# A state-space block with a gated MLP: the residual's addition given to accumulating DMAs, and the sums of one layer norm moved

## The chip, the cores and the metric

The kernel runs on one core of a Trainium2 chip. The metric is the device time of one execution in microseconds (us). A core has five engines with a queue each, which execute in order and meet through semaphores: TensorE (PE in the profile: matmuls, with weight loads PEld), VectorE (DVE), ScalarE (ACT), GpSimd (POOL), and SyncE (SP), which here only issues DMAs. Matmuls write PSUM, a small memory which the other engines must empty; all else lies in SBUF.

## The reference

The input x has 2048 rows of 512. It is normalized, and the normalized rows feed a diagonal complex recurrence with 512 states and a gated MLP of width 1792; the result is the sum of x and both branches.

```python
xn = _layernorm(x)                      # over 512, eps 1e-5, no gain
dt = exp(log_dt); Lam_bar = exp(dt * Lam)
B_bar = ((Lam_bar - 1.0) / Lam)[:, None] * Bmat
Bu = einsum("bld,pd->blp", xn, B_bar)
h[t] = Lam_bar * h[t - 1] + Bu[t]       # 2048 steps, complex
ssm = 2.0 * einsum("blp,dp->bld", h, Cmat).real + xn * Dskip
mlp = (silu(xn @ w1) * (xn @ w3)) @ w2
return x + ssm + mlp                    # bfloat16, [1, 2048, 512]
```

## The kernel before

The 2048 rows are cut into four blocks of 512 (four tiles of 128 rows each, `cl` 0 to 3). For each block b the work is:

- layer norm: rows of `x_blk[b]` become `xn_blk[b]`, and DMA transposes on SP (`ln_transpose`, L239) make `xnT_blk[b]` from it. There are three forms. Block 0 and block 1 use DVE; blocks 2 and 3 use ACT (`ln_scalar_engine`, L259): for each of the four row tiles a sum of x (`total`, L269), a sum of squared deviations (`squares`, L274) and the normalization (`norm`, L282). ACT's instructions give the sums through an accumulator, but each also has an elementwise result, which goes into the place of xn and is overwritten later. POOL makes the mean from the sums (L271), and then the reciprocal deviation (L277 to L279).
- `bu(b)`: 32 matmuls into two PSUM tiles in turn (`bu_ps`), each evacuated by ACT (L424) for the scans.
- `ssm_tasks(b)`: on DVE, a rotation, eight scans (L456) and a rotation back.
- `glu(b)`: 14 pairs of a gate and an up tile (L497, four PSUM tiles `gu_ps`), evacuated by ACT (L506, L507) and multiplied by DVE (L514).
- `res_tasks(b)`: on DVE, xn times Dskip (`mul`, L590), plus x (`add`, L594), in place of xn, and for blocks 1 to 3 a `difference` (L598), which the fast output needs.
- the output: for block 0 `y(0)`, whose four PSUM tiles are first seeded with the residual by ACT (`y_seed`, L749), then filled by `from_gate` (L756) and `from_state` (L762), and copied and stored by `finish` (L768, L769). Blocks 1 to 3 use `y_fast` (L674), a seven-product scheme on pairs of row tiles, which takes sums of activations made by DVE (`row_sums`, L649), and is seeded by ACT (`seeds`, L671).

The order on each engine is the order in which the Python code emits instructions; no scheduler reorders them. Two queues decide at emission what is interleaved. `bg`, a `Filler`, holds DVE work as (cost, function, key); `bg.fill(budget)`, called after matmuls, emits tasks as far as the budget goes, and `bg.flush(key)` emits all up to the last with this key. `sins` holds single ACT operations, and `sin_step()` emits one of them; the calls stand in `bu` (L425) and once in each pair of `glu` (L581).

Before the change, `ln_scalar_engine(2)` is emitted all at once ahead of `y(0)`; `ln_scalar_engine(3, sins)` puts its twelve ACT operations into `sins` behind `y(0)`, so that they are taken one by one in bu(2) and in the pairs of glu(2). The buffer of xn for a block is allocated (`ln_alloc`) at that call, out of three; the one for block 3 is that of block 0, which `y(0)` stores from.

PSUM is fully dealt out: four `gu_ps`, two `bu_ps` and two `y_ps` tiles of 512 float32 columns. `y_ps` serves the first transposes and, from output pair 1 on, half of the fast outputs.

Of the kernel before, what the change touches and what calls it, by code (L numbers as in the profile page):

```python
# [11 lines left out]
ALU = mybir.AluOpType  # L12
ACT = mybir.ActivationFunctionType

FP32 = DT.float32
BF16 = DT.bfloat16
FP16 = DT.float16
P = 128
# [44 lines left out]
def kernel(  # L63
# [17 lines left out]
    nc = tc.nc  # L81
    _, S, D = A_x.shape
# [16 lines left out]
    FAST = (1, 2, 3)  # L99
# [18 lines left out]
    ps_y = ctx.enter_context(tc.tile_pool(name="ps_y", bufs=2, space=bass.MemoryType.PSUM))  # L118
# [24 lines left out]
    x_blk = [xpool.tile([P, CPB, D], BF16, name="x_blk") for _ in range(NBLK)]  # L143
# [59 lines left out]
    bg = Filler()  # L203


    xn_blk = [None] * NBLK
# [12 lines left out]
    def ln_alloc(b):  # L219
        xn_blk[b] = lnp.tile([P, CPB, D], BF16, name="xn", bufs=3)  # L220
        xnT_blk[b] = xtp.tile([P, NDT, TBLK], BF16, name="xnT")
# [16 lines left out]
    def ln_transpose(b, cl):  # L238
        nc.sync.dma_start_transpose(out=xnT_blk[b][:, :, cl * P:(cl + 1) * P], in_=xn_blk[b][:, cl, :])  # L239
# [18 lines left out]

    def ln_scalar_engine(b, spread=None):  # L259

        ln_alloc(b)
        acc = lnp.tile([P, 4, CPB], FP32, name="acc")
        sm, nm, ss, nb = (acc[:, i, :] for i in range(4))
        rstd = rstd_all[:, b * CPB:(b + 1) * CPB]
        xn, gp = xn_blk[b], nc.gpsimd
        todo = []

        def total(cl):
            nc.scalar.activation(out=xn[:, cl, :], in_=x_blk[b][:, cl, :], func=ACT.Copy, accum_out=sm[:, cl:cl + 1])  # L269
            if cl == CPB - 1:  # L270
                gp.tensor_scalar(out=nm, in0=sm, scalar1=-1.0 / D, scalar2=None, op0=ALU.mult)  # L271

        def squares(cl):
            nc.scalar.activation(out=xn[:, cl, :], in_=x_blk[b][:, cl, :], func=ACT.Square, bias=nm[:, cl:cl + 1],  # L274
                                 scale=1.0, accum_out=ss[:, cl:cl + 1])
            if cl == CPB - 1:
                gp.tensor_scalar(out=ss, in0=ss, scalar1=1.0 / D, scalar2=LN_EPS, op0=ALU.mult, op1=ALU.add)  # L277
                gp.tensor_tensor(out=rstd, in0=ss, in1=mhalf, op=ALU.pow)
                gp.tensor_tensor(out=nb, in0=nm, in1=rstd, op=ALU.mult)  # L279

        def norm(cl):
            nc.scalar.activation(out=xn[:, cl, :], in_=x_blk[b][:, cl, :], func=ACT.Identity,  # L282
                                 bias=nb[:, cl:cl + 1], scale=rstd[:, cl:cl + 1])
            ln_transpose(b, cl)

        for fn in (total, squares, norm):
            for cl in range(CPB):
                if spread is None:
                    fn(cl)
                else:  # L290
                    spread.append((None, lambda fn=fn, cl=cl: fn(cl)))
# [13 lines left out]
    gp = nc.gpsimd  # L305
# [25 lines left out]
    sins = deque()  # L331
    sins_done = set()

    def sin_step(until=None):
        while sins and (until is None or until not in sins_done):
            key, fn = sins.popleft()
            fn()
            sins_done.add(key)
            if until is None:
                break  # L340
# [55 lines left out]
    def k_gate(f):  # L396
        return f if f < NFH else NK + f - NFH
# [4 lines left out]
    def act(b):  # L402
        if act_blk[b] is None:
            act_blk[b] = actp.tile([P, 2 * NK, TBLK], FP16, name="act")
        return act_blk[b]
# [7 lines left out]
    def bu(b):  # L413
        for hf in range(NPT // 2):
            u = up.tile([P, 2, 2, TBLK], BF16, name="u")
            u_blk[b, hf] = u
            for j in range(2):
                pt = 2 * hf + j
                for ri in range(2):
                    ps = ps_bu.tile([P, TBLK], FP32, name="bu_ps")  # L420
                    for dt in range(NDT):
                        nc.tensor.matmul(out=ps, lhsT=bt[:, ri, dt, pt * P:(pt + 1) * P], rhs=xnT_blk[b][:, dt, :],  # L422
                                         start=(dt == 0), stop=(dt == NDT - 1))
                    nc.scalar.activation(out=u[:, j, ri, :], in_=ps, func=ACT.Copy)  # L424
                if (b == 0 and pt > 0) or b == 1 or (b == 2 and pt > 1):  # L425
                    sin_step()
            bg.fill(3.4)

# [159 lines left out]
    def res_tasks(b):  # L588
        def mul():
            nc.vector.tensor_tensor(out=xn_blk[b], in0=xn_blk[b],  # L590
                                    in1=dskip_row[:, None, :].to_broadcast([P, CPB, D]), op=ALU.mult)

        def add():
            nc.vector.tensor_tensor(out=xn_blk[b], in0=xn_blk[b], in1=x_blk[b], op=ALU.add)  # L594

        def difference():
            o = xn_blk[b]
            nc.vector.tensor_tensor(out=o[:, 0::2, D2].bitcast(FP16), in0=o[:, 0::2, D2], in1=o[:, 1::2, D2],  # L598
                                    op=ALU.subtract)

        bg.add(1.2, mul)
        bg.add(1.2, add, ("res", b))
        if b in FAST:
            bg.add(0.4, difference, ("res", b))

    def weight_state(kh, dsl):
        return ct[:, kh * NPH:(kh + 1) * NPH, :, dsl].rearrange("p a r d -> p (a r) d")
# [22 lines left out]
    def sum_homes():  # L630
        n = NK * P
        flat = [bt.rearrange("p r t d -> p (r t d)"), w1_sb.rearrange("p t f -> p (t f)"),
                w3_sb.rearrange("p t f -> p (t f)")]
        b0, b1, a0, a1, a2, a3 = (v[:, i * n:(i + 1) * n] for v, m in zip(flat, (2, 2, 2)) for i in range(m))
        xs = [x_blk[i].rearrange("p c d -> p (c d)")[:, 0:n] for i in range(2)]
        q = flat[0][:, 2 * n:2 * n + 4 * DH].bitcast(FP32).rearrange("p (i d) -> p i d", d=DH)
        q_last = flat[1][:, 4 * n:4 * n + 2 * DH].bitcast(FP32)
        return [xs, [b0, b1], [b0, b1], [a0, a1], [a2, a3], xs], q, q_last
# [3 lines left out]
    def row_sums(n, b, p):  # L642
        a = act(b)
        r1, r2 = slice(2 * p * P, (2 * p + 1) * P), slice((2 * p + 1) * P, (2 * p + 2) * P)
        a11, a12 = a[:, 0:NK, r1], a[:, NK:2 * NK, r1]
        a21, a22 = a[:, 0:NK, r2], a[:, NK:2 * NK, r2]
        s1, s2 = (v.bitcast(FP16).rearrange("p (k t) -> p k t", t=P) for v in homes[n])
        sums[n] = dict(a11=a11, a12=a12, a22=a22, s1=s1, s2=s2, s3=a21)
        return [(0.9, lambda out=out, x=x, z=z, op=op: nc.vector.tensor_tensor(out=out, in0=x, in1=z, op=op), ("sums", n))  # L649
                for out, x, z, op in ((s1, a21, a22, ALU.add), (a21, a11, a21, ALU.subtract),  # L650
                                      (s2, s1, a11, ALU.subtract))]
# [99 lines left out]
    def y(b):  # L751
        tiles = y_tiles

        def from_gate(cl):
            for f in range(NFT):
                nc.tensor.matmul(out=tiles[cl], lhsT=act_blk[b][:, k_gate(f), cl * P:(cl + 1) * P],  # L756
                                 rhs=w2_sb[:, f, :], start=False, stop=False, skip_group_check=True)

        def from_state(cl):
            for ri in range(2):  # L760
                for pt in range(NPT):
                    nc.tensor.matmul(out=tiles[cl], lhsT=act_blk[b][:, k_state(pt, ri), cl * P:(cl + 1) * P],  # L762
                                     rhs=ct[:, pt, ri, :], start=False, stop=(ri == 1 and pt == NPT - 1),
                                     skip_group_check=True)

        def finish(cl):
            o = xn_blk[b][:, cl, :]
            nc.scalar.activation(out=o, in_=tiles[cl], func=ACT.Copy)  # L768
            nc.sync.dma_start(out=ov[:, b * CPB + cl, :], in_=o)  # L769

        for cl in range(0, CPB, 2):
            from_gate(cl)
            bg.fill(3.2)
            from_gate(cl + 1)
            bg.fill(3.2)
            if cl == 0:
                bg.flush(("ssm", b))
            from_state(cl)
            finish(cl)
            bg.fill(1.6)  # L780
            from_state(cl + 1)
            finish(cl + 1)
            bg.fill(1.6)
# [33 lines left out]
    y_seed(0, 2)  # L817
    y_seed(0, 3)
    ln_scalar_engine(2)
    y(0)  # L820
    pairs = [(b, p) for b in FAST for p in range(CPB // 2)]
    homes, q, q_last = sum_homes()
    for t in row_sums(0, *pairs[0]):
        bg.add(*t)
    ssm_tasks(2)
    ln_scalar_engine(3, sins)
    bu(2)
    gate = glu(2)
    gate()
# [4 lines left out]
    posts = ssm_tasks(3, True)  # L834
    y_fast(0, row_sums(1, *pairs[1]))
    y_fast(1, row_sums(2, *pairs[2]))
    posts()
    res_tasks(3)
    gate = glu(3)
    gate()  # L840
    bg.settle()
# [36 lines left out]
```

## Time and profile before

| | |
|---|---|
| median of 8 runs | 208.81 us (208.16 to 209.84) |
| the profiled execution | 208.84 us |
| its span | 207.0 us, so 1.84 us lie around it |
| granted TensorE clock | 1.00 |
| TensorE / DVE / ACT / POOL busy | 201.2 / 181.6 / 128.9 / 25.5 us |
| matmuls with 512 columns | 0.217 us each where they follow one another |

Times in the views are us from the start of the span. A timeline line gives the start, the length, the engine, the line of the code, the operation, out<-in, the number of merged instructions, and in brackets how long the engine had been idle before it and what ended that. A line of the waits gives who waited for whom, the total, the number of times and the longest. Rows last longer than the distance between starts, since instructions overlap at their ends.

The course of the span: block 0's layer norm, bu and glu up to 63 us with glu(1) at its end; bu(1) from 63.2; output 0 from 70.5 to 89.7; bu(2) from 89.9; glu(2) from 96.8; bu(3) from 122.2; the first two fast outputs from 129.1; glu(3) from 145.9; the last four fast outputs from 170.1.

### The profile page before, as it was taken

How to read it: one execution, taken by the hardware profiler on the slowest of the kernel's cores; microseconds unless marked ns; L12 is line 12 of the kernel's file. 1: busy time of each engine (PE TensorE's matmuls, PEld its weight loads, DVE VectorE, ACT ScalarE, POOL GpSimd, SP SyncE). 2: the span in 40 equal slices, each digit the busy share in tenths (PEclk: the TensorE clock that was granted, in tenths of full speed). 3: DMA queues.
4: the chain of work that ended last, by engine and by line, in shares of the span. 5: the costliest groups of instructions: out<-in, count | busy, mean ns of one | idle time of the engine just before them, and what ended most of it. 6: DMA issues, size and time to landing. Idle time of an engine off the chain costs nothing.

```text
span 207.0 us, 3249 instructions
## 1 busy us (share of the span) xinstructions
PE 201.2 (97%) x1251; PEld 115.8 (56%) x1251; DVE 181.6 (88%) x236; ACT 128.9 (62%) x257; POOL 25.5 (12%) x47
## 2 busy tenths in 40 slices
PE   8999999999999999999997999999999999999994
PEld 2774444444444444444443444888544458888893
DVE  3789699999997899999996889896999999996932
ACT  3799788699999984558995986300466672011010
POOL 3250289300000014000006000000000000000000
DMA  6999997930000000540000410000100000101011
GB/s 173 261 277 191 319 176 176 302 136 0 0 3 0 0 0 0 79 127 2 0 0 0 79 25 0 0 30 24 52 3 0 0 0 3 51 0 54 25 40 41
DMA packets 26103, 13.71 MB, mean 66 GB/s; under 512 B 15720, under 2 KB 26088, under 8 KB 26088
## 3 DMA queue, kind: packets, MB, share of 16 engines
q1 hardware_dynamic: 25512, 13.21, 26.6%
q10 hardware_dynamic: 576, 0.30, 0.5%
q8 instruction: 10, 0.16, 0.3%
q14 instruction: 5, 0.04, 0.1%
HBM read 7.74 MB, written 2.10 MB: 48 GB/s over the span
## 4 chain that ended last, share of the span: by engine, by line
PE 69%; DVE 20%; DMA 4%; ACT 3%; POOL 1%; issue 1%; SPq 0%; ACTq 0%; POOLq 0%
PE gu_ps L497 37%; PE gu_ps L690 11%; PE y_ps L690 7%; PE bu_ps L422 7%; PE bu_ps L690 6%; DVE u L456 5%; DVE u L446 2%; DVE p L443 2%; DVE tw L625 2%; DMA w_sb<-in_B_w_dram 2%; DVE u L450 2%; DMA x_blk<-in_A_x_dram 1%; DVE p L461 1%; DVE act L468 1%; DVE act L464 1%; ACT u L424 1%
## 5 line engine op out<-in xcount | busy, mean ns | idle before, releaser
L497 PE MATMUL gu_ps<-xnT,w_sb 128*128 128x512 bf16 x424 | 92.3, 379 | 1.1 <-ACT g L506 1.1
L497 PEld LDWEIGHTS <-w_sb 128*128 128x128 bf16 x424 | 41.4, 98 | 50.9 <-issue 1.4
L506 ACT ACTIVATE g<-gu_ps 128x512 bf16<-128x512 f32 x55 | 33.1, 603 | 10.8 <-PE gu_ps L497 10.6
L507 ACT ACTIVATE u<-gu_ps 128x512 bf16<-128x512 f32 x55 | 33.3, 605 | 6.8 <-PE gu_ps L497 5.9
L690 PEld LDWEIGHTS <-act 128*128 128x128 f16 x341 | 32.4, 98 | 4.3 <-DVE act L722 0.2
L456 DVE TENSOR_TENSOR_SCAN u<-rho,act,u 128x512 bf16<-128x512 f32 x24 | 29.3, 1266 | 0.0
L422 PE MATMUL bu_ps<-xnT,bt 128*128 128x512 bf16 x128 | 28.8, 379 | 0.4 <-DMA xnT<-xn 0.2
L424 ACT ACTIVATE u<-bu_ps 128x512 bf16<-128x512 f32 x32 | 19.1, 596 | 5.8 <-PE bu_ps L422 5.7
L514 DVE TENSOR_TENSOR act<-g,u 128x1024 f16<-128x1024 bf16 x28 | 19.0, 680 | 3.9 <-ACT u L507 3.9
L422 PEld LDWEIGHTS <-bt 128*128 128x128 bf16 x128 | 12.4, 98 | 16.2 <-issue 1.0
L756 PE MATMUL gu_ps<-w_sb,act 128*128 128x512 bf16 x56 | 12.4, 379 | 0.0
L446 DVE TENSOR_TENSOR u<-u,tabe 128x2048 bf16<-128x2048 bf16 x8 | 9.8, 1221 | 0.1
L443 DVE TENSOR_TENSOR p<-u,tabe 128x2048 bf16<-128x2048 bf16 x8 | 9.8, 1220 | 0.1
L461 DVE TENSOR_TENSOR p<-u,tabe 128x2048 bf16<-128x2048 bf16 x8 | 9.8, 1220 | 0.1
L468 DVE TENSOR_TENSOR act<-act,p 128x2048 f16<-128x2048 f16 x8 | 9.7, 1217 | 0.1
L450 DVE TENSOR_TENSOR u<-u,p 128x2048 bf16<-128x2048 bf16 x8 | 9.8, 1219 | 0.0
L464 DVE TENSOR_TENSOR act<-u,tabe 128x2048 f16<-128x2048 bf16 x8 | 9.7, 1217 | 0.0
L282 ACT ACTIVATE xn<-x_blk,acc,rstd_all 128x512 bf16<-128x512 bf16 x8 | 6.2, 811 | 5.3 <-POOL acc L279 5.3
L456 DVE TENSOR_TENSOR_SCAN u<-rho,u 128x512 bf16<-128x512 f32 x8 | 9.2, 1207 | 0.1
L756 PEld LDWEIGHTS <-act 128*128 128x128 f16 x56 | 5.5, 98 | 6.6
L703 ACT ACTIVATE bu_ps<-y_ps 128x256 f32<-128x256 f32 x3 | 1.1, 368 | 11.9 <-PE y_ps L690 11.9
L703 ACT ACTIVATE gu_ps<-gu_ps 128x256 f32<-128x256 f32 x3 | 1.1, 368 | 11.7 <-PE gu_ps L690 11.7
(136 smaller groups left out, 258.2 us busy)
## 6 DMA issues: line engine op xcount, KB each, us to landing
out_dram<-xn SPq DMA_DIRECT2D x15, 128.0 KB, 1.7
w_sb<-in_B_w_dram SPq DMA_DIRECT2D x1, 1792.0 KB
x_blk<-in_A_x_dram SPq DMA_DIRECT2D x3, 512.0 KB, 8.9
w_sb<-in_B_w_dram SPq DMA_DIRECT2D x2, 768.0 KB, 6.7
w_sb<-in_B_w_dram SPq DMA_DIRECT2D x4, 256.0 KB, 3.9
w_sb<-in_B_w_dram SPq DMA_DIRECT2D x2, 512.0 KB, 6.4
xnT<-xn SPq DMA_TRANSPOSE x12, 3.2
x_blk<-in_A_x_dram ACTq DMA_DIRECT2D x2, 64.0 KB
```

The costliest lines, as they stand in the source:

```text
L422: nc.tensor.matmul(out=ps, lhsT=bt[:, ri, dt, pt * P:(pt + 1) * P], rhs=xnT_blk[b][:, dt, :], start=(dt == 0), stop=(dt == NDT - 1))
L424: nc.scalar.activation(out=u[:, j, ri, :], in_=ps, func=ACT.Copy)
L443: nc.vector.tensor_tensor(out=st["p"], in0=st["g"], in1=tabe[:, psl, 1:3, :], op=ALU.mult)
L446: nc.vector.tensor_tensor(out=st["g"], in0=st["g"], in1=tabe[:, psl, 0:1, :].to_broadcast(FULL), op=ALU.mult)
L450: nc.vector.tensor_tensor(out=st["g"], in0=st["g"], in1=st["p"][:, :, ::-1, :], op=ALU.subtract)
L456: nc.vector.tensor_tensor_scan(out=v, data0=rho[:, pt:pt + 1].to_broadcast([P, TBLK]), data1=v, initial=init, op0=ALU.mult, op1=ALU.add)
L497: nc.tensor.matmul(out=ps[:, tsl], lhsT=w[:, dt, f * P:(f + 1) * P], rhs=xnT[:, dt, tsl], start=(dt == 0), stop=(dt == NDT - 1))
L506: nc.scalar.activation(out=g16[:, f % 2, :], in_=g_ps, func=ACT.Silu)
L507: nc.scalar.activation(out=u16[:, f % 2, :], in_=u_ps, func=ACT.Copy)
L514: nc.vector.tensor_tensor(out=act(b)[:, k0:k1 + 1:k1 - k0, :], in0=g16, in1=u16, op=ALU.mult)
L690: nc.tensor.matmul(out=out, lhsT=left[:, k, :], rhs=right[k][:, cols], start=(start and k == 0), stop=(k == NK - 1), skip_group_check=True)
L756: nc.tensor.matmul(out=tiles[cl], lhsT=act_blk[b][:, k_gate(f), cl * P:(cl + 1) * P], rhs=w2_sb[:, f, :], start=False, stop=False, skip_gr ...
```

## The change

There are two parts.

The residual's addition. `add` is no longer a DVE instruction: it is a DMA issued from GpSimd's queue which adds `x_blk[b]` (512 KB in bfloat16) to `xn_blk[b]` in place, in SBUF. It is a `bg` task of cost 0, issued behind `mul`. `difference` becomes a function of its own, `res_difference`, called later: for block 1 behind output 0's scheduling, for block 2 and block 3 around the scans' last part. `res_tasks(3)` is called before `posts()`.

Layer norm 3. `ln_scalar_engine(3, sins)` is called ahead of `y(0)`. `y(0)` takes two operations of `sins` behind each `from_gate`, so the four totals come in the first half of output 0 and the four squares in the second; the norms come in glu(2). bu(2) takes none any more. In both `ln_scalar_engine` calls the elementwise results of `total` and `squares` go to `y_ps` tiles, and the buffer of xn is allocated at the first norm.

```diff
     def ln_scalar_engine(b, spread=None):
-        ln_alloc(b)
...
-        xn, gp = xn_blk[b], nc.gpsimd
-        todo = []
+        gp = nc.gpsimd
         def total(cl):
-            nc.scalar.activation(out=xn[:, cl, :], in_=x_blk[b][:, cl, :], func=ACT.Copy, accum_out=sm[:, cl:cl + 1])
+            nc.scalar.activation(out=ps_y.tile([P, D], FP32, name="y_ps"), in_=x_blk[b][:, cl, :], func=ACT.Copy,
+                                 accum_out=sm[:, cl:cl + 1])
...
         def squares(cl):
-            nc.scalar.activation(out=xn[:, cl, :], in_=x_blk[b][:, cl, :], func=ACT.Square, bias=nm[:, cl:cl + 1],
-                                 scale=1.0, accum_out=ss[:, cl:cl + 1])
+            nc.scalar.activation(out=ps_y.tile([P, D], FP32, name="y_ps"), in_=x_blk[b][:, cl, :], func=ACT.Square,
+                                 bias=nm[:, cl:cl + 1], scale=1.0, accum_out=ss[:, cl:cl + 1])
...
         def norm(cl):
+            if cl == 0:
+                ln_alloc(b)
...
-                if (b == 0 and pt > 0) or b == 1 or (b == 2 and pt > 1):
+                if (b == 0 and pt > 0) or b == 1:
                     sin_step()
...
         def add():
-            nc.vector.tensor_tensor(out=xn_blk[b], in0=xn_blk[b], in1=x_blk[b], op=ALU.add)
+            gp.dma_start(out=xn_blk[b], in_=x_blk[b], accum_op=ALU.add)
+
+        bg.add(1.2, mul)
+        bg.add(0.0, add, ("res", b))
+
+    def res_difference(b):
         def difference():
...
-        bg.add(1.2, mul)
-        bg.add(1.2, add, ("res", b))
-        if b in FAST:
-            bg.add(0.4, difference, ("res", b))
+        bg.add(0.4, difference, ("res", b))
...
         for cl in range(0, CPB, 2):
-            from_gate(cl)
-            bg.fill(3.2)
-            from_gate(cl + 1)
-            bg.fill(3.2)
+            for c in (cl, cl + 1):
+                from_gate(c)
+                sin_step()
+                sin_step()
+                bg.fill(3.2)
...
     ln_scalar_engine(2)
+    ln_scalar_engine(3, sins)
     y(0)
     pairs = [(b, p) for b in FAST for p in range(CPB // 2)]
     homes, q, q_last = sum_homes()
+    res_difference(1)
     for t in row_sums(0, *pairs[0]):
         bg.add(*t)
     ssm_tasks(2)
-    ln_scalar_engine(3, sins)
     bu(2)
...
     y_fast(1, row_sums(2, *pairs[2]))
+    res_tasks(3)
+    res_difference(2)
     posts()
-    res_tasks(3)
+    res_difference(3)
     gate = glu(3)
```

More of the change, by code (lines that the diff above doesn't have):

```diff
@@ L281, in norm @@
         def norm(cl):
-            nc.scalar.activation(out=xn[:, cl, :], in_=x_blk[b][:, cl, :], func=ACT.Identity,
+            if cl == 0:
+                ln_alloc(b)
+            nc.scalar.activation(out=xn_blk[b][:, cl, :], in_=x_blk[b][:, cl, :], func=ACT.Identity,
                                  bias=nb[:, cl:cl + 1], scale=rstd[:, cl:cl + 1])
```

## The prediction

> **What bounds the kernel now.** I read the page first, for the engine that carries the span.
>
> ```profile
> PE 201.2 (97%) x1251; PEld 115.8 (56%) x1251; DVE 181.6 (88%) x236; ACT 128.9 (62%) x257; POOL 25.5 (12%) x47
> ...
> PE 69%; DVE 20%; DMA 4%; ACT 3%; POOL 1%; issue 1%; SPq 0%; ACTq 0%; POOLq 0%
> ```
>
> TensorE is busy for 201.2 of 207.0 us. The change leaves its matmuls and their order alone, so it can only win or lose where TensorE stands still. DVE's 20% of the chain is a hint, not a limit: TensorE has matmuls to do beside it. Next, the waits: TensorE's own are these.
>
> ```profile
> PE gu_ps L497 <- ACT g L506: 1.1, 1, 1.1
> ...
> PE bu_ps L422 <- DMA xnT<-xn: 0.2, 1, 0.2
> ```
>
> The first is the only stall worth the name. TensorE's timeline places it, and shows the work on both sides dense (72 matmuls in 15.70 us, 0.217 us each, as elsewhere):
>
> ```profile
> 86.04 3.62 PE L762 MATMUL gu_ps<-ct,act 128*128 128x512 f16 x16
> 89.87 7.08 PE L422 MATMUL bu_ps<-xnT,bt 128*128 128x512 bf16 x32 [0.21 <-DMA xnT<-xn]
> 96.78 15.70 PE L497 MATMUL gu_ps<-xnT,w_sb 128*128 128x512 bf16 x72
> 113.59 8.79 PE L497 MATMUL gu_ps<-xnT,w_sb 128*128 128x512 bf16 x40 [1.10 <-ACT g L506]
> ```
>
> Then ACT's and POOL's timelines at that place, to see who is late.
>
> ```profile
> 109.07 0.60 ACT L507 ACTIVATE u<-gu_ps 128x512 bf16<-128x512 f32 x1
> 112.24 0.81 ACT L282 ACTIVATE xn<-x_blk,acc,rstd_all 128x512 bf16<-128x512 bf16 x1 [2.57 <-POOL acc L279]
> 112.96 0.58 ACT L506 ACTIVATE g<-gu_ps 128x512 bf16<-128x512 f32 x1
> ```
>
> ```profile
> 108.72 1.13 POOL L277 TENSOR_SCALAR acc<-acc 128x4 f32<-128x4 f32 x1 [6.67 <-ACT xn L274]
> 109.93 1.94 POOL L278 TENSOR_TENSOR rstd_all<-acc,mhalf 128x4 f32<-128x4 f32 x1
> ```
>
> ACT executes in order. Norm 3 (L282) waits 2.57 us for POOL's three small operations, and the evacuations of the gate tiles stand behind it; all four gu_ps tiles fill, and TensorE stops for 1.10 us. Last, ACT where the sums are to go:
>
> ```profile
> 72.75 0.62 ACT L269 ACTIVATE xn<-x_blk 128x512 bf16<-128x512 bf16 x1
> ...
> 75.11 0.19 ACT L269 ACTIVATION_READ_ACCUMULATOR xn<-x_blk 128x1 f32 x1
> 76.01 0.72 ACT L274 ACTIVATE xn<-x_blk,acc 128x512 bf16<-128x512 bf16 x1 [0.71 <-POOL acc L271]
> ...
> 78.76 0.19 ACT L274 ACTIVATION_READ_ACCUMULATOR xn<-x_blk,acc 128x1 f32 x1
> 81.70 2.93 ACT L282 ACTIVATE xn<-x_blk,acc,rstd_all 128x512 bf16<-128x512 bf16 x4 [2.76 <-POOL acc L279]
> 84.53 1.06 ACT L768 ACTIVATE xn<-gu_ps 128x512 bf16<-128x512 f32 x2
> 87.97 0.60 ACT L768 ACTIVATE xn<-gu_ps 128x512 bf16<-128x512 f32 x1 [2.38 <-PE gu_ps L762]
> 89.69 0.60 ACT L768 ACTIVATE xn<-gu_ps 128x512 bf16<-128x512 f32 x1 [1.13 <-PE gu_ps L762]
> 90.94 0.60 ACT L424 ACTIVATE u<-bu_ps 128x512 bf16<-128x512 f32 x1 [0.65 <-PE bu_ps L422]
> 91.81 0.60 ACT L424 ACTIVATE u<-bu_ps 128x512 bf16<-128x512 f32 x1 [0.27 <-PE bu_ps L422]
> ```
>
> Between the end of norm 2 and the first evacuation of bu(2), ACT idles 2.38+1.13+0.65 = 4.2 us. That is the hole for the moved sums.
>
> **Part 1: layer norm 3 moved.** The built order shows it: ACT now has norm 2, four totals of block 3, finish 0 and 1, four squares, finish 2 and 3, eight evacuations of bu(2), and then one norm 3 behind each of the first four gate/up pairs. TensorE's order is unchanged.
>
> What goes: norm 3 no longer waits, because POOL's rstd has some 5 us before it is wanted. A pair with a norm takes ACT 1.66 us (norms start at 113.92 and 115.58) against TensorE's eight matmuls of 1.73 us, so ACT keeps up. −1.10 us.
>
> What comes: four totals took 72.75 to 75.30 = 2.55 us; four squares 76.01 to 78.94 = 2.93, of which 2.84 until the next can start. Starting at 84.53, totals end at 87.08; finish 0 and 1 (0.97 until the next) end at 87.95. POOL's mean starts at 87.16 and took 0.33 (block 3) to 0.59 (block 2); its sibling L277 took up to 1.13, so it is ready at 87.5 to 88.3. Squares start at 87.95 to 88.33 and free ACT at 90.8 to 91.2; TensorE's tiles for finish 2 and 3 are done by 89.7, so these follow at once, and the first evacuation of bu(2) starts at 91.76 to 92.14 instead of 90.94. The work (5.4+1.9 us) does not fit the hole entirely: **the new wait is here**. bu(2) has two bu_ps tiles; its groups of four matmuls take 0.865 us and end at 90.90 and 91.76, and the third needs the first tile back: 91.76+0.60 = 92.36 to 92.74. TensorE stalls 0.63 to 1.0 us, say 0.75. Afterwards ACT's 0.50 per evacuation catches up with 0.865 per group, so this is paid once.
>
> The writes go to y_ps (two tiles). TensorE uses none between its parameter transposes at 7 us and output 2 at 137.5, so nobody waits for them. Here the Trainium skill has a rule in favour: "ScalarE: Activation LUTs", section "Step-by-step: what each stage is for", calls PSUM the lower-latency target of an activation. The rows: a copy to PSUM (L749) and one to SBUF (L269) last 594 and 619 ns, but both let the next instruction start after 0.52 us (L749 at 71.19, three in 1.63; L269 at 72.75, its read at 73.27). By the rule 16 operations would save 16 x 25 ns = 0.4 us; by the starts, nothing. I take the starts.
>
> Of the moved norms, the four transposes on SP go from 113 to about 99 us, ahead of no other transfer, and are wanted at 122. The norms write the buffer that output 0's stores read; the last store leaves at about 92.5 and lands in the listed 1.7 us, 4 us before the first norm. The totals write PSUM, so they no longer wait for that. Sum of part 1: −1.10+0.75 = −0.35 us (−0.47 to −0.10).
>
> **Part 2: four DVE adds become accumulating DMAs.** DVE loses 4 x 1.22 = 4.9 us. The profile gives this no value: adds 0 and 1 stand at 55.9 and 61.5, and DVE then waits 1.78 us at 68.27 for ACT's scaled weights (L383), so it only waits longer. The adds of blocks 2 and 3 stand where TensorE is dense. If that cover were gone, the last add would hold up only L722 at 183.7, for which TensorE was 0.03 us late: −0.03 at most. Difference 1 is moved to 96.9 (0.42 us of DVE, before row sums wanted at 130); mul and difference of later blocks change places with other DVE work: 0.
>
> The waits that come: seed 0 of output 0 (ACT L749, 69.25) for the first DMA, whose mul ends at 55.84: **13.4 us** of cover. Behind that seed stand ACT's last two evacuations of bu(1) and all of layer norm 2. The DMA for block 1 follows mul 1 (ends near 61) and is wanted near 97, for block 2 132 against 165, block 3 about 165 against 180. On POOL, layer norm 2's mean (75.38) is queued behind the first two, layer norm 3's behind nothing more.
>
> No DMA from POOL's queue and no accumulation is in the trace. Bounds: below, 3.2 us, an estimate by the fit 2.0+bytes/436e3 of the Trainium skill, "DMA: Bandwidth & Descriptors", section "Anatomy of one DMA" (524,288 bytes). The nearest row is a load of the same 512 KB, 8.9 us with others in flight. I take 8.9: landing at 64.8, 4.4 us early, cost 0. From above comes a rule of the Trainium skill against this change: "SBUF — State Buffer", section "Summary: rules for kernel authors", says not to hide a DMA of GpSimd's queue under DVE, since its descriptors starve while DVE runs in fast modes; its section "A bandwidth-pool intuition that's wrong" gives 620 against 3100 ns. Five times 3.2 would be 16 us: seed 0 at 71.9, 2.6 late, and the sum would be +2.3 rather than −0.35. But the same page ("Who interferes with whom") exempts tensor_tensor from the port lock that blocks writes, and every DVE row from 54 to 64 us is TENSOR_TENSOR. Hence 0, with up to +2.6 kept for the range; a gain is excluded, since nothing waited for the adds.
>
> **Sum.** On the profiled execution (208.84 us = 207.0 span + 1.84 around it): 208.84−0.35 = 208.49. It stands 0.03 above the median of eight runs, so 208.5 as a median too.
>
> **The rivals.**
>
> *A (0.55), above:* the wait changes place, 208.5 (208.3 to 208.75 by its terms).
>
> *B (0.25), the hole is large enough:* ACT reaches bu(2) by 91.1, the stall is gone. For it: 0.7 us is a small gap, and a shorter chain of norm 2 on POOL (its L277 ranges 0.34 to 1.13 us) would move ACT forward and take up to 0.2 us of the xnT wait too. Against it: the sum of rows above. −1.1 to −1.3: 207.6.
>
> *C (0.13), slower by the residual's DMA:* from a landing later than 69.25, i.e. 13.4 us after mul 0, each us stops ACT, two bu_ps tiles fill, and TensorE stops with it. For it: no row shows such a DMA, and the rule above. Against it: DMA engines that the page's GB/s row shows idle from 47 to 83 us. At 16 us: 208.5+2.6 = 211.1.
>
> *D (0.07), POOL as the bound:* DVE's scan at 87.33 (1.27 us) blocks POOL's mean for its whole length, or descriptor writing slows DVE and POOL. The squares then start some 0.9 us later, bu(2) stalls 1.7 us: −1.10+1.7 = +0.6, about 209.4.
>
> That the change doesn't do what it says is excluded by the built order: DVE lacks the four adds, POOL has four DMA issues, ACT's sums stand ahead of finish 0 and 2.
>
> **How the numbers follow.** About 0.3% (0.63 us) is what a measurement of this kernel can tell from no change. Faster by more: B, and 0.05 of A's lower edge = 0.30. Slower by more: C, D's upper half (0.05) and 0.05 for A with terms mis-sized upward = 0.23. Within: 0.47. The range reaches down through B (207.6) and up through D (209.5), and leaves out C's late landings and B's tail.
>
> **What would show it.** Right: TensorE's 1.10 us at L497 gone; a wait of 0.6 to 1.0 us at the third group of bu(2) released by ACT's evacuation; first evacuation at about 91.9; ACT's first seed not waiting for a DMA; POOL's DMAs landing within 10 us. Wrong: no wait at bu(2) (B); ACT's seed released by the DMA (C); squares waiting for POOL over 0.4 us (D); layer norm 2's chain later than 84.5 us.

## The result, and the profile after

| | before | after |
|---|---|---|
| median | 208.96 us of 53 runs (208.05 to 210.03) | 208.04 us of 18 runs (207.66 to 208.75) |
| profiled execution, its span | 208.84, 207.0 us | 207.88, 206.1 us |

The ratio is 0.996, 95% interval 0.9948 to 0.9972: 0.84 us less (0.58 to 1.09 of 208.96). It is formed from the single runs and is not quite the quotient of the medians, which lie 0.92 us apart. It is a small gain: its middle lies beyond the prediction's 0.3%, the end of the interval nearest to no change (0.28%) just inside. The runs of before include those made beside the experiments.

The page of the changed kernel: engines, the chain that ended last by engine, the new group of DMA issues, and their landing (KB each, us from issue to landing).

```profile
PE 201.3 (98%) x1251; PEld 116.2 (56%) x1251; DVE 176.7 (86%) x232; ACT 129.8 (63%) x257; POOL 29.4 (14%) x51
...
PE 84%; ACT 11%; POOL 2%; DVE 1%; issue 1%
...
L595 POOL DMA_DIRECT2D xn<-x_blk x4 | 3.7, 935 | 91.2 <-DVE xn L591 91.2
...
xn<-x_blk POOLq DMA_DIRECT2D x4, 512.0 KB, 4.9
```

TensorE's work is the same (201.3 us, 201.2 before). DVE lost 4.9 us of work and went from 20% of the chain to 1%, which looks large and is worth next to nothing. The chain's share does not even follow the adds: it is 1% in experiment 1 below, where they are still on DVE, and 22% in experiment 5, at the same time for the whole. The chain passed through DVE, but DVE was not what TensorE waited for. ACT's and POOL's shares rose, since the chain now passes through layer norm 3's sums in output 0.

TensorE's timeline where the prediction has its stalls:

```profile
85.75 3.62 PE L764 MATMUL gu_ps<-ct,act 128*128 128x512 f16 x16
89.49 1.90 PE L423 MATMUL bu_ps<-xnT,bt 128*128 128x512 bf16 x8
92.05 5.34 PE L423 MATMUL bu_ps<-xnT,bt 128*128 128x512 bf16 x24 [0.66 <-ACT u L425]
97.23 24.34 PE L498 MATMUL gu_ps<-xnT,w_sb 128*128 128x512 bf16 x112
121.40 7.07 PE L423 MATMUL bu_ps<-xnT,bt 128*128 128x512 bf16 x32
```

Before, bu(3) began later:

```profile
122.22 7.07 PE L422 MATMUL bu_ps<-xnT,bt 128*128 128x512 bf16 x32
```

glu(2) now runs its 112 matmuls in one go: the 1.10 us stall is gone. In its place bu(2) stops behind its first eight matmuls, at the third group, until ACT gives back the first `bu_ps` tile. The wait for xnT ahead of bu(2) no longer has a bracket, but bu(2) starts 3.74 us after the last products of output 0, whose 16 matmuls need 16 x 0.217 = 3.47: it was still about 0.28 late. (In some of the traces a few records of matmuls are missing: a row can count 7 where 8 ran, or 110 for 112.)

ACT's timeline at the same place (the lines left out are more of the same operations):

```profile
81.41 2.93 ACT L283 ACTIVATE xn<-x_blk,acc,rstd_all 128x512 bf16<-128x512 bf16 x4 [2.76 <-POOL acc L278]
84.24 0.58 ACT L267 ACTIVATE y_ps<-x_blk 128x512 f32<-128x512 bf16 x1
...
86.69 1.05 ACT L770 ACTIVATE xn<-gu_ps 128x512 bf16<-128x512 f32 x2
87.64 0.68 ACT L273 ACTIVATE y_ps<-x_blk,acc 128x512 f32<-128x512 bf16 x1
...
90.46 1.06 ACT L770 ACTIVATE xn<-gu_ps 128x512 bf16<-128x512 f32 x2
91.42 1.06 ACT L425 ACTIVATE u<-bu_ps 128x512 bf16<-128x512 f32 x2
93.11 0.60 ACT L425 ACTIVATE u<-bu_ps 128x512 bf16<-128x512 f32 x1 [0.63 <-PE bu_ps L423]
```

From 81.41 to the first evacuation of bu(2) at 91.42 there is no bracket: ACT is never idle. The old holes (2.38, 1.13 and 0.65 us) are full, and the first evacuation of bu(2) comes so late that TensorE stops. Ahead of that, ACT still waits 2.76 us for POOL before norm 2, untouched by the change.

How much the stalls really cost is read from start to start, since a row of a matmul lasts 379 ns where the next one begins after 217: a gap between rows hides 0.16 us. "Dense" is the time that the stretch takes where its matmuls follow one another.

| stretch of TensorE's timeline | before | after | difference |
|---|---|---|---|
| last products of output 0 to bu(2), dense 3.47 | 3.83 | 3.74 | −0.09 |
| bu(2) to glu(2), dense 6.9 | 6.91 | 7.74 | +0.83 |
| glu(2) to bu(3), dense 24.2 | 25.44 | 24.17 | −1.27 |
| one group of eleven at L690 (after: L692), near 183 us | 1.33 | 1.21 | −0.12 |
| sum | | | −0.65 |
| from bu(1)'s start to the end of the span | 143.84 | 143.22 | −0.62 |

Spans are given to 0.1 us, so the last line is good to about 0.1.

bu(1) itself began at 63.16 us before and at 62.88 after. That start lies at 62.45 to 63.57 us in the nine profiled executions of this study, in an order that follows no edit. It is later where TensorE waited longer for the weights' DMA in block 0 (less than 0.2 us in the changed kernel, 0.2 before, 0.8 in experiment 7, 1.0 in experiment 3). So 0.28 us of the profiled difference is not credited to the change. The last line of the table is the measure that the experiments use below.

### The profile page after: what moved, and what is told of

The parts are those of the page before. It is cut to its first block, busy times and chain, and to the rows that moved or that the text cites. A ratio compares the mean times of both kernels' runs of the same rounds, so it can differ in the third digit from the quotient of the medians.

```text
span 206.1 us, 3270 instructions
## 1 busy us (share of the span) xinstructions
PE 201.3 (98%) x1251; PEld 116.2 (56%) x1251; DVE 176.7 (86%) x232; ACT 129.8 (63%) x257; POOL 29.4 (14%) x51
## 3 DMA queue, kind: packets, MB, share of 16 engines
HBM read 7.74 MB, written 2.10 MB: 48 GB/s over the span
## 4 chain that ended last, share of the span: by engine, by line
PE 84%; ACT 11%; POOL 2%; DVE 1%; issue 1%
PE gu_ps L498 44%; PE gu_ps L692 11%; PE bu_ps L423 10%; PE y_ps L692 7%; PE bu_ps L692 6%; ACT y_ps L273 3%; ACT y_ps L267 2%; PE bu_ps L190 2%; PE gu_ps L529 2%; ACT u L425 2%; ACT xn L283 1%; PE bu_ps L529 1%; ACT xn L770 1%; POOL rstd_all L277 1%; ACT gu_ps L751 1%
## 5 line engine op out<-in xcount | busy, mean ns | idle before, releaser
L507 ACT ACTIVATE g<-gu_ps 128x512 bf16<-128x512 f32 x55 | 33.0, 601 | 13.0 <-PE gu_ps L498 12.9
L692 PEld LDWEIGHTS <-act 128*128 128x128 f16 x341 | 32.5, 98 | 4.0
L595 POOL DMA_DIRECT2D xn<-x_blk x4 | 3.7, 935 | 91.2 <-DVE xn L591 91.2
```

The source lines that it names most:

```text
L507: nc.scalar.activation(out=g16[:, f % 2, :], in_=g_ps, func=ACT.Silu)
L692: nc.tensor.matmul(out=out, lhsT=left[:, k, :], rhs=right[k][:, cols], start=(start and k == 0), stop=(k == NK - 1), skip_group_check=True)
```

## The experiments

Experiments 1 to 4 were timed against before on one chip (before: 208.78 us, median of 23 runs), experiments 5 to 7 on another (timed runs of before there: 208.68). A ratio is formed from the single runs against those of before, with its 95% interval; it can differ from the quotient of the medians (by 0.0013 in experiment 6).

**1. Layer norm 3 alone.** Before, with only the second part of the change (PSUM results, totals and squares in output 0, norms in glu(2)); the residual's additions stay on DVE.

```diff
-        ln_alloc(b)
...
+            for c in (cl, cl + 1):
+                from_gate(c)
+                sin_step()
+                sin_step()
+                bg.fill(3.2)
...
+    ln_scalar_engine(3, sins)
     y(0)
```

> Layer norm 3's part alone; the residual's additions stay on DVE. Theory (the gain is ACT's queue): the 1.27 us that TensorE loses at the gate tiles of glu(2) goes, 0.83 us comes at the third group of bu(2), the wait for xnT is 0.1 us shorter: -0.54 us against the kernel before, ratio 0.9974, and L722 at 184 us still holds TensorE up by 0.12 us. Rival (the relief of DVE makes the gain): ratio 1.000. Rival (part of it was the start of the profiled execution, which was 0.28 us earlier): the start differs from run to run and not with the kernel.

207.87 us, ratio 0.9955 (0.9936 to 0.9973), more gain than was expected; from bu(1) to the end 143.25 us, 0.59 less than before, close to the expected 0.54. TensorE's timeline:

```profile
85.33 3.62 PE L763 MATMUL gu_ps<-ct,act 128*128 128x512 f16 x16
88.78 1.67 PE L423 MATMUL bu_ps<-xnT,bt 128*128 128x512 bf16 x7
91.63 5.34 PE L423 MATMUL bu_ps<-xnT,bt 128*128 128x512 bf16 x24 [1.18 <-ACT u L425]
```

The layer norm part carries the gain, as far as a timing can tell. The stall at bu(2) is longer here (1.18 against 0.66), because bu(2) began without a wait for xnT, 3.45 us behind the last products. The third group begins 6.30 us behind those products in both kernels (85.33 to 91.63, 85.75 to 92.05): ACT's backlog sets that time, and a wait for xnT ahead of it costs nothing more. The new stall and that wait are therefore one term: from the last products to glu(2) it is 11.48 us in both kernels, against 10.74 before.

**2. The accumulating DMAs alone.** Before, with only the first part.

```diff
-            nc.vector.tensor_tensor(out=xn_blk[b], in0=xn_blk[b], in1=x_blk[b], op=ALU.add)
+            gp.dma_start(out=xn_blk[b], in_=x_blk[b], accum_op=ALU.add)
...
+        bg.add(1.2, mul)
+        bg.add(0.0, add, ("res", b))
```

> The residual's part alone; layer norm 3 stays in bu(2) and glu(2) and its sums write xn. Theory: only the 0.12 us at 184 us (TensorE waiting for L722 behind DVE's mul, add and difference of block 3) goes: ratio 0.9994, the stall of 1.10 us in glu(2) is unchanged. Rival (DVE's relief makes the gain): ratio 0.996. DMAs land in 5 to 6.2 us, and no seed waits for them.

208.71 us, ratio 1.0 (0.9981 to 1.0019); from bu(1) to the end 143.63 us, 0.21 less. The stall of before is still there, and late in the span DVE now waits for TensorE (the second view, DVE's timeline):

```profile
113.48 8.79 PE L497 MATMUL gu_ps<-xnT,w_sb 128*128 128x512 bf16 x39 [1.04 <-ACT g L506]
```

```profile
180.74 0.42 DVE L602 TENSOR_TENSOR xn<-xn 128x512 f16<-128x512 bf16 x1
182.21 0.89 DVE L723 TENSOR_TENSOR act<-act,w_sb 128x1408 f16<-128x1408 f16 x1 [1.05 <-PE gu_ps L691]
```

Before, this last operation (there L722) came straight behind the last addition and its difference, and TensorE's next group waited for it: 1.33 us from 183.32 to 184.65, where 1.21 are dense. The lines of before, DVE's and TensorE's:

```profile
183.37 0.43 DVE L598 TENSOR_TENSOR xn<-xn 128x512 f16<-128x512 bf16 x1
183.71 0.88 DVE L722 TENSOR_TENSOR act<-act,w_sb 128x1408 f16<-128x1408 f16 x1
```

```profile
183.32 1.36 PE L690 MATMUL gu_ps<-tw,act 128*128 128x256 f16 x11
184.65 0.94 PE L690 MATMUL gu_ps<-w_sb,act 128*128 128x256 bf16 x7
```

With the DMAs DVE waits 1.05 us for TensorE instead, and the group takes 1.20. So 4.9 us less of DVE bought some 0.12 us, less than a timing can show.

**3. Totals into ACT's other wait.** If the overflow is ACT's, it should go when work is moved into the 2.76 us that ACT spends waiting for POOL before norm 2. The changed kernel, with block 3's four totals between squares 2 and norm 2, and only the squares left in output 0.

```diff
-    ln_scalar_engine(2)
-    ln_scalar_engine(3, sins)
+    for fn in total2 + squares2 + total3 + norm2:
+        fn()
+    sins.extend((None, fn) for fn in squares3 + norm3)
...
-                sin_step()
-                sin_step()
+                if cl:
+                    sin_step()
+                    sin_step()
```

> The four totals of block 3 are put into ACT's wait for POOL in layer norm 2 (2.76 us; they take 2.45), ahead of norm 2, and the four squares behind finish 0 and 1. Theory (the new wait at bu(2) is ACT's backlog): ACT is free for bu(2) 2.4 us earlier, so the 0.83 us at its third group goes: ratio 0.992 (0.996 - 0.004). Norm 2 is not later, since totals end at 81.0 and POOL is ready at 81.4. Rival (norm 2 comes later or another wait takes the place, such as transposes): 0.996 again.

207.35 us, ratio 0.9927 (0.9902 to 0.9951); from bu(1) to the end 142.45 us, 1.39 less than before. TensorE's and ACT's timelines:

```profile
90.20 7.08 PE L417 MATMUL bu_ps<-xnT,bt 128*128 128x512 bf16 x31 [0.15 <-DMA xnT<-xn]
97.12 24.34 PE L492 MATMUL gu_ps<-xnT,w_sb 128*128 128x512 bf16 x110
```

```profile
82.08 2.93 ACT L283 ACTIVATE xn<-x_blk,acc,rstd_all 128x512 bf16<-128x512 bf16 x4 [0.31 <-POOL acc L278]
84.92 1.05 ACT L764 ACTIVATE xn<-gu_ps 128x512 bf16<-128x512 f32 x2
85.87 0.68 ACT L273 ACTIVATE y_ps<-x_blk,acc 128x512 f32<-128x512 bf16 x1
```

The same four operations, begun at 79.23 instead of 84.24 us, cost nothing: the wait for POOL shrinks from 2.76 to 0.31 us, and bu(2) runs dense. The cause of the new stall is shown: it is the amount of work on ACT between norm 2 and bu(2), and not the writes to PSUM or the DMAs, which this kernel has too.

**4. The seeds too.** Experiment 3 with output 0's seeds 2 and 3 also put into that wait, with three of the totals; the fourth total follows norm 2. Layer norm 2 then comes 1.04 us earlier, which should also end the wait for xnT.

```diff
+    seeds23 = [lambda: y_seed(0, 2), lambda: y_seed(0, 3)]
+    for fn in total2 + squares2 + seeds23 + total3[:3] + norm2 + total3[3:]:
+        fn()
```

> As before it, and seeds 2 and 3 of output 0 also go into that wait (with three totals; the fourth follows norm 2), so that layer norm 2 starts 1.04 us earlier. Theory: xnT of block 2 is there 1 us earlier, TensorE's 0.28 us wait ahead of bu(2) goes as well: ratio 0.9905 to 0.991. Rival (seeds late for output 0's matmuls at 79.7 us, or the transposes not bound by the norms): 0.992 or above.

207.39 us, ratio 0.9934 (0.9912 to 0.9956); from bu(1) to the end 142.85 us. Less gain than expected. The wait for xnT is gone, but the stall at bu(2) is back, for neither of the reasons that the expectation named. TensorE's, ACT's, POOL's and DVE's timelines:

```profile
92.23 5.34 PE L417 MATMUL bu_ps<-xnT,bt 128*128 128x512 bf16 x24 [0.78 <-ACT u L419]
```

```profile
87.81 0.69 ACT L273 ACTIVATE y_ps<-x_blk,acc 128x512 f32<-128x512 bf16 x1 [2.51 <-POOL acc L270]
```

```profile
84.43 3.35 POOL L270 TENSOR_SCALAR acc<-acc 128x4 f32<-128x4 f32 x1 [3.66 <-ACT y_ps L267]
```

```profile
84.22 1.20 DVE L445 TENSOR_TENSOR u<-u,p 128x2048 bf16<-128x2048 bf16 x1
85.34 1.21 DVE L456 TENSOR_TENSOR p<-u,tabe 128x2048 bf16<-128x2048 bf16 x1
86.47 1.22 DVE L459 TENSOR_TENSOR act<-u,tabe 128x2048 f16<-128x2048 bf16 x1
87.61 1.27 DVE L451 TENSOR_TENSOR_SCAN u<-rho,act,u 128x512 bf16<-128x512 f32 x1
```

POOL's mean, sixteen bytes a row, took 3.35 us instead of 0.33 and held ACT's squares back by 2.51. It began 0.21 us behind the start of the first of these DVE operations and ended at 87.78, just behind the start of the fourth. This is rival D of the prediction in kind: POOL late, and ACT with it. The timed runs do not tell this kernel from experiment 3 (207.39 and 207.35 us); the stall is seen in the one profiled execution, which was the slowest of its six runs (208.07).

**5. DVE copies over the first DMA.** The changed kernel with eight copies of 128x512 float32 on DVE right behind `mul` 0, over the issue of the first accumulating DMA, to try the rule that rival C rests on.

```diff
+            if b == 0:
+                for _ in range(8):
+                    nc.vector.tensor_copy(out=slot32[6], in_=slot32[5])
```

> The kernel after, with eight DVE copies of 128x512 float32 (unused scratch) right behind block 0's mul, while POOL makes the descriptors of the first accumulating DMA. In the kernel after, beside TENSOR_TENSOR alone, that issue took 1.08 us on POOL and landed 6.2 us later (the other three 0.86 to 0.94). If copies starve descriptor making, as a rule weighed in the prediction has it, the first issue lasts until the copies end (some 2.5 to 4 us) and lands that much later; if not, 1.1 and 6.2 us. Either way it lands before 69 us and the time stays within 0.3% of the kernel after.

One run: 207.97 us. POOL's issue lies inside the row of copies:

```profile
55.56 3.75 DVE L598 COPY tw<-tw 128x512 f32<-128x512 f32 x8
```

```profile
55.96 1.13 POOL L595 DMA_DIRECT2D xn<-x_blk  x1 [18.25 <-DVE xn L591]
```

The issue took 1.13 us, against 1.08 in the changed kernel, and the longest time to landing is 6.2 us in both. These copies held up neither the issue nor the landing.

**6. The means on ACT.** Experiment 4 with the means of blocks 2 and 3 made by ACT itself, so that no small POOL operation lies between totals and squares.

```diff
-                gp.tensor_scalar(out=nm, in0=sm, scalar1=-1.0 / D, scalar2=None, op0=ALU.mult)
+                nc.scalar.activation(out=nm, in_=sm, func=ACT.Copy, scale=-1.0 / D)
```

> The kernel with totals and seeds 2 and 3 in ACT's gap, but the means of blocks 2 and 3 (128x4) are computed on ACT instead of POOL. Theory: there POOL's mean of block 3 lasted 3.35 us beside three DVE TENSOR_TENSORs, ended 0.17 us after DVE's scan began, and held ACT up by 2.51 us, which gave the stall of 0.95 us at bu(2); without POOL in that step squares follow finish 1 at once and the stall goes: ratio 0.989 to 0.991. Rival (ACT is late for bu(2) for another reason, or xnT is): 0.993 again, with a TensorE wait at bu(2) of 0.5 us or more.

206.79 us (median of 8 runs, 206.47 to 208.28), ratio 0.9922 (0.9897 to 0.9947): a little less gain than the expected 0.989 to 0.991, which lies partly within the interval. From bu(1) to the end 142.14 us, 1.70 less than before. TensorE's and ACT's timelines:

```profile
89.19 7.07 PE L417 MATMUL bu_ps<-xnT,bt 128*128 128x512 bf16 x32
96.09 24.34 PE L492 MATMUL gu_ps<-xnT,w_sb 128*128 128x512 bf16 x112
```

```profile
83.79 0.21 ACT L270 ACTIVATE acc<-acc 128x4 f32<-128x4 f32 x1
83.90 1.07 ACT L764 ACTIVATE xn<-gu_ps 128x512 bf16<-128x512 f32 x2
84.86 0.69 ACT L273 ACTIVATE y_ps<-x_blk,acc 128x512 f32<-128x512 bf16 x1
```

Neither stall is left between output 0 and bu(3). This is the best version that was run, faster than before and most likely than the change itself, though the two intervals only just miss each other (0.9947, 0.9948); against experiments 3 and 4 they overlap.

**7. Probing POOL beside DVE.** Was it DVE that stretched the mean in experiment 4? The changed kernel with forty more copies of it, behind block 3's last small operation, where POOL has nothing to do.

```diff
+                for _ in range(40 if b == 3 else 0):
+                    gp.tensor_scalar(out=nm, in0=sm, scalar1=-1.0 / D, scalar2=None, op0=ALU.mult)
```

> The changed kernel with forty more copies of POOL's mean of block 3 (128x4 f32, the same operation and tensors; the value written is the same and nobody waits for it), put behind block 3's last small operation on POOL, which ended at 94.3 us in the changed kernel. They probe how long this operation lasts beside each kind of DVE instruction: from 94.3 to 106.7 us DVE runs two-input TENSOR_TENSOR almost without a gap, from 106.7 to 115 scans and TENSOR_TENSOR in turn, from 120.7 to 122.2 it idles. Theory 1 (a two-input TENSOR_TENSOR keeps POOL from its operands): copies under back-to-back TENSOR_TENSOR last 1 to 3.5 us, their ends lie within 0.3 us of a scan's start or of a gap of DVE, and copies under scans or in a gap last under 0.6 us. Theory 2 (the scan keeps POOL out): copies under a scan last as long as what is left of it, those under TENSOR_TENSOR 0.3 us. Theory 3 (the 3.35 us were not DVE's doing, but came with the operation's place in its chain): all copies last 0.2 to 0.6 us. The time stays within 0.5 us of the changed kernel's by all three, since POOL has nothing to do until 131 us; by theory 1 the copies end between 110 and 128 us, by theory 3 before 116.

One run: 208.6 us beside 208.9 of before; from bu(1) to the end 143.23 us, as in the changed kernel. Some of the forty on POOL's timeline, then DVE's timeline at the same times (rows of narrow windows; what lies between is left out):

```profile
109.99 1.05 POOL L280 TENSOR_SCALAR acc<-acc 128x4 f32<-128x4 f32 x1
...
114.56 1.10 POOL L280 TENSOR_SCALAR acc<-acc 128x4 f32<-128x4 f32 x1
115.75 1.05 POOL L280 TENSOR_SCALAR acc<-acc 128x4 f32<-128x4 f32 x1
...
121.84 0.22 POOL L280 TENSOR_SCALAR acc<-acc 128x4 f32<-128x4 f32 x1
122.14 0.22 POOL L280 TENSOR_SCALAR acc<-acc 128x4 f32<-128x4 f32 x1
```

```profile
109.75 2.45 DVE L459 TENSOR_TENSOR_SCAN u<-rho,act,u 128x512 bf16<-128x512 f32 x2
...
114.38 1.20 DVE L453 TENSOR_TENSOR u<-u,p 128x2048 bf16<-128x2048 bf16 x1
115.50 1.22 DVE L464 TENSOR_TENSOR p<-u,tabe 128x2048 bf16<-128x2048 bf16 x1
...
122.94 0.69 DVE L517 TENSOR_TENSOR act<-g,u 128x1024 f16<-128x1024 bf16 x1 [1.57 <-ACT u L510]
```

In DVE's pause before 122.94 the operation takes 0.22 us. Beside a scan and beside a TENSOR_TENSOR alike it takes 1.05 to 1.24, and ends shortly behind the start of the next DVE instruction: 114.56+1.10 = 115.66, DVE's next began at 115.50. So POOL's small operation lasts as long as DVE's instruction beside it lets it. (In experiment 3 the mean of block 3 lasted 1.24 us too, beside scans; nobody waited for it.) No theory was right as it stood: scans hold it too, which the first excluded, and TENSOR_TENSOR as well, which the second did. The longest of the forty is 1.24 us, one DVE instruction; why the mean of experiment 4 missed two such boundaries and ended at the third stays open.

## Why the prediction was right

The likeliest case, A, came as described: the wait at glu(2) went, and a smaller one came at bu(2). Its sign and its place held; its size was too small. Neither −0.62 us (from bu(1) to the end) nor −0.84 (by the ratio) lies within A's own terms, −0.47 to −0.10, and a change within 0.3% was held likelier (0.47) than the larger gain (0.30) that the ratio's middle shows. The stated range held the result because it reached down to 207.6 for case B, which did not come: that much of it is luck. By steps:

- *Norm 3 no longer waits, −1.10.* Right in kind, undersized. The step took the gap between two rows (1.10) as the stall; from start to start it is 1.27. The norms take ACT no longer than TensorE's eight matmuls, but with nothing to spare: pairs with a norm follow at 1.72 to 1.73 us on ACT (100.36, 102.08, 103.81, 105.54 at L507), where 1.66 was worked out, and TensorE runs dense.
- *The hole is too small, +0.75.* Right: 0.66 as a gap between rows, +0.83 from start to start, +0.74 with the wait for xnT ahead of it, which is part of it (experiment 1). The working had the mean start at 87.16 and the first evacuation come at 91.76 at the earliest; less the 0.28 us by which bu(1) began earlier in this execution, these are 86.88 and 91.48, and they came at 86.87 and 91.42. Experiments 1 and 3 show that this stall belongs to ACT's work in output 0 alone.
- *PSUM as a target saves nothing.* Right: L267 lasts 577 to 591 ns against 616 to 622 of L269, so the rows are shorter, as the rule weighed in the prediction has it, but totals still follow every 0.61 us, squares every 0.70, as before. The rule holds here for the length of a row, not for the rate.
- *The adds on DVE are worth 0.* Right to what a timing shows (ratio 1.0, experiment 2). The bound on the last add, "−0.03 at most", was too tight: −0.12, because TensorE's small gap hides again behind the length of a row.
- *The DMAs are hidden.* Right. The two first landed within 6.2 us, where 13.4 us of cover were there; the taken 8.9 was too high, the estimate of 3.2 too low. No seed waited for one. POOL's issue, which the sum had at nothing, took 0.86 to 1.08 us each, and nobody waited for it.
- *The sum.* −0.35 was forecast, −0.62 is what the stretch from bu(1) to the end shows, and −0.84 (−1.09 to −0.58) what the ratio does, whose interval holds −0.62. The terms that were off, from start to start: −0.17 for the old stall's real size, +0.08 for the new one, −0.09 for the wait for xnT ahead of it and −0.12 for L722, together −0.30; −0.27 is to be explained, and the 0.03 between them is below what the rows resolve. Reading gaps for stalls did little harm to the pair: the hidden 0.16 us stands in the old stall and in the new one, so gap against gap gives −1.10+0.66 = −0.44 and start against start −1.27+0.83 = −0.44.

Of the rivals, B (no stall at bu(2)) did not come by itself: experiment 3's reordering brought it about, and gave −1.39 us from bu(1) to the end, where B had −1.1 to −1.3 (about 0.12 of it is L722's). C is excluded in this kernel by the landings; experiment 5 saw no starvation, but with one kind of copy only. D did not come, but its mechanism is there: in the changed kernel the mean began at 86.87, 0.17 us before DVE's next instruction at 87.04, and so was through after 0.33 us. POOL's line and DVE's:

```profile
86.87 0.33 POOL L270 TENSOR_SCALAR acc<-acc 128x4 f32<-128x4 f32 x1 [5.50 <-ACT y_ps L267]
```

```profile
87.04 1.27 DVE L457 TENSOR_TENSOR_SCAN u<-rho,act,u 128x512 bf16<-128x512 f32 x1
```

In experiment 4 it met the wrong moment. Where D went wrong is that it named the scan only: in experiments 4 and 7 TENSOR_TENSOR does it as well. What the prediction weighed in TENSOR_TENSOR's favour, for the DMA's issue, does not carry over to this small operation.

## What to carry to other kernels

Work that one engine has to do before a consumer with few buffers is not free because the engine idles there: add up the rows, and see whether the sum ends before the consumer's last free buffer is full. Here a wait of the same engine a few microseconds earlier was the better place: moving the totals there about doubled the gain (−1.39 against −0.62 us). A tiny operation on POOL between two steps of a chain can cost what DVE happens to be doing; where the engine that waits for it can do it itself in 0.2 us, as ACT did in experiment 6, that is safer.

## What the runs showed of the hardware

A POOL operation on 128x4 float32 takes 0.22 us while DVE stands still and 1.05 to 1.24 us beside DVE instructions of 1.2 us, one of POOL's for each of DVE's (experiment 7); once it took 3.35 us (experiment 4). The rows of those DVE instructions stayed at 1.20 to 1.28 us meanwhile.

An accumulating DMA of 512 KB within SBUF, from POOL's queue, took 0.86 to 1.13 us of POOL and landed in 4.5 to 6.2 us.
